# Loading a transformer block's condition and beta as rows and spreading them with TensorE products

## Chip, cores and metric

The kernel runs on one core of a Trainium2 chip. The metric is the device time of one execution in microseconds (us). The core has five engines that run side by side, each in its own order: TensorE (PE in the profile, its weight loads PEld), VectorE (DVE), ScalarE (ACT), GpSimd (POOL) and SyncE (SP). SP and ScalarE also issue DMA transfers; these issues stand in the timeline as SPq and ACTq, and the transfers of the two queues run on the core's 16 DMA engines as q1 (SP) and q10 (ScalarE).

## The reference

A transformer block over 2048 rows of 512 features, with adaptive layer norms. A condition `c` of 512 numbers gives six vectors of 512 that shift, scale and gate the two halves of the block:

```
mod = (silu(c) @ w_mod).reshape(1, 6, 1, 512)     # sa, ca, ga, sb, cb, gb
h = layernorm(x) * (1 + ca) + sa
x = x + ga * A(h)          # 32 heads, 4 segments of 512 rows, softmax attention and a running memory
h = layernorm(x) * (1 + cb) + sb
x = x + gb * ((h @ w_gate) * (h @ w_up)) @ w_down
g = sigmoid(beta)          # inside A: one gate per head, o = g * a_mem + (1 - g) * a_dot
```

So nothing of the attention can be computed before `silu(c)`, its product with the first 1024 columns of `w_mod` (for `sa` and `ca`) and the layer norm of the first segment. `beta`, 32 numbers, is wanted later, when memory and attention are mixed.

## The kernel before, in words

The kernel is one long program without loops on the chip. Attention runs over 4 segments, 4 groups of 8 heads and 2 halves of a group; projections, memory updates and the second half of the block are woven between the attention steps. TensorE's order is written by hand: `MM` (line 84) and `TP` (line 87) chain every product and transpose to the one before. VectorE and ScalarE have such chains too in the opening part: what is called through `CV` and `CA` (line 90) keeps the order of the program text; the profile gives all of these line 39. `pin` ties a DMA or an operation to TensorE's last instruction in the same order, without a wait.

The change lies in the opening part, which runs once. In the order of the text:

- Line 628: ScalarE issues the load of the condition. The host has laid `c` out as 128 rows of 4 (line 1670), and it arrives as a tile `s_c` of 128 partitions by 4 columns, 16 bytes for each partition.
- Line 643: SP issues the first four tiles of `x`, 128 by 512 each. Line 665: it issues the first half of the modulation weights, four tiles `wm0` of 256 KB (`wm0_load(0)`); the second half follows by `wm0_load(1)` (line 1103), after the first key weights (line 759). Line 774 issues four tiles of value weights.
- Lines 648 to 657: 18 products of 512 columns of a tile of zeros, `wu`, into the PSUM tile `wups`, which nobody reads: work that warms TensorE up. `wups` has two banks; the products fill the first.
- Line 669: ScalarE issues the load of `beta`, spread by the DMA over all 128 partitions, 128 bytes to each, into `be`.
- Lines 670 to 673: silu. ScalarE computes exp(-c); VectorE adds 1, takes the reciprocal and multiplies by c, in place in `s_c`.
- Line 675: four fills on GpSimd of rows of the tiles `kst`, tied behind the last of these operations.
- `gates` (line 677) uses `be` for the two sigmoids, `gg` and `omg`. Line 680 is its exponential on ScalarE.
- `ln` (line 172): for each of four tiles of `x` VectorE computes statistics (`bn_stats`) and joins them (`bn_aggr`, line 182); then follow two operations on ScalarE, four small ones on VectorE, and the normalisation of the four tiles. Sixteen transposes on TensorE (line 209, by way of line 88) put the result in PSUM as `atp`.
- `mod0` (line 719) multiplies the modulation weights by `s_c`, four blocks of 128 columns and four parts of the condition, with the moving column repeated 96 times (`MW`); an f32 product is two instructions. `mod0(0)` stands on TensorE ahead of the transposes, `mod0(1, (1, 2, 3))` behind them; the latter takes its first two parts as one sum that ScalarE (line 1109) and VectorE (line 1112) make beforehand.
- Then `a_kq` computes the first keys and queries (`kps`, `qps`), and the block proper begins.

Storage that is used by turns goes by tags: a tile that takes a tag whose buffer is in use waits for the last reader. The tags `mem` and `pkr` of the pool `pa`, one buffer each, serve the value weights in this part and parts of the memory update later.

Of the kernel before, what the change touches and what calls it, by code (L numbers as in the profile page):

```python
# [8 lines left out]
F32 = mybir.dt.float32  # L9
F32R = mybir.dt.float32r  # L10
BF = mybir.dt.bfloat16
AF = mybir.ActivationFunctionType
# [5 lines left out]
P = 128  # L18
S, D, H, DH, NSEG, L, F = 2048, 512, 32, 16, 4, 512, 1376
KT = D // P  # L20
# [6 lines left out]
ONES2 = 1.0 + 0x3F80 / 2.0 ** 23  # L27
SYNC = mybir.DependencyInfo(mybir.DependencyClass.Sync, mybir.DependencyReason.DATA)
# [29 lines left out]
def tile_kernel(ctx, tc, x, wq, wk_, wv, wo, beta, w_gate, w_up, w_down, c, w_mod, out):  # L58
    nc = tc.nc
# [3 lines left out]
    def open_pool(**kw):  # L63
        p = tc.tile_pool(**kw)
        return p, p.__enter__()
# [6 lines left out]
    def pe(i):  # L72

        if last_pe[0] is not None:
            tc.add_manual_dep(i.ins, last_pe[0].ins.name, NOSYNC, reason="order")
        last_pe[0] = i
        return i

    def pin(i):

        if last_pe[0] is not None:
            tc.add_manual_dep(i.ins, last_pe[0].ins.name, NOSYNC, reason="order")

    def MM(*a, **k):
        return pe(nc.tensor.matmul(*a, **k))  # L85

    def TP(*a):
        return pe(nc.tensor.transpose(*a))

    CV, CA = Chain(tc, nc.vector), Chain(tc, nc.scalar)  # L90
    vec, act = Switch(nc.vector), Switch(nc.scalar)
# [35 lines left out]
    def bank(name, dt=F32, shape=(P, 512), small=False):  # L127

        flush()
        rest_of()  # L130
        nbank[0] += 1
        tag = btag[nbank[0] % len(btag)]
        if tag == "ms":
            if not small:
                nlast[0] ^= 1
            tag = f"ms{nlast[0] ^ int(small)}"
        return pst(shape, tag, name, dt)
# [4 lines left out]
    ones = cst.tile([P, P], F32, name="ones")  # L142
# [14 lines left out]
    s_c = cst.tile([P, KT], F32, name="s_c")  # L157
    be = cst.tile([P, H], F32, name="be")
    e1 = cst.tile([P, KT], F32, name="e1")
# [12 lines left out]
    def ln(pool, hpool, xt, s, sc, sh, pfx, hb, fast):  # L172

        first = pfx == "a" and s == 0
        V, A = (CV, CA) if first else (vec, act)
        mv = pool.tile([P, 4, 2], F32, tag="mv", name=f"{pfx}mv{s}", bufs=2)
        for t in range(4):
            st = pool.tile([P, 6], F32, tag="st", name=f"{pfx}st{s}_{t}", bufs=2)
            i = V.bn_stats(st, xt[t])
            if not first:  # L180
                pin(i)
            V.bn_aggr(mv[:, t, :], st)
            if not first:
                yield 0.0
        sd = pool.tile([P, 4], F32, tag="sd", name=f"{pfx}sd{s}", bufs=2)
        A.activation(sd, mv[:, :, 1], AF.Ln, bias=epst[:, 0:1])
        y = pool.tile([P, 4], F32, tag="y", name=f"{pfx}y{s}", bufs=2)
        A.activation(y, sd, AF.Exp, scale=-0.5)
        a = pool.tile([P, 4], F32, tag="ya", name=f"{pfx}ya{s}", bufs=2)
        b = pool.tile([P, 4], F32, tag="yb", name=f"{pfx}yb{s}", bufs=2)  # L190
        eng = CV if first else nc.gpsimd
        eng.tensor_mul(a, y, y)
        if first:
            CV.scalar_tensor_tensor(b, mv[:, :, 1], EPS, a, op0=ALU.add, op1=ALU.mult)
        else:
            eng.tensor_scalar(b, mv[:, :, 1], 1.0, EPS, op0=ALU.mult, op1=ALU.add)
            eng.tensor_mul(b, b, a)
        eng.tensor_scalar(b, b, -0.5, 1.5, op0=ALU.mult, op1=ALU.add)
        eng.tensor_mul(y, y, b)
        yield 0.0  # L200
        tps = [bank(f"{pfx}tp{s}_{d}") for d in range(KT)] if first else []
        for t in range(4):
            i = V.tensor_scalar(xt[t], xt[t], mv[:, t, 0:1], y[:, t:t + 1],
                                op0=ALU.subtract, op1=ALU.mult)
            if not first:
                pin(i)
                yield 0.0
            for d, ps in enumerate(tps):
                TP(ps[:, t * P:(t + 1) * P], xt[t][:, d * P:(d + 1) * P], ident)
        if first:  # L210
            yield 0.0
        hH, hL = [], []
        if first:
            hcur[0] = hH, hL
        for d in range(KT):
            if first:
                ps = tps[d]
            else:
                ps = bank(f"{pfx}tp{s}_{d}", small=pfx == "c" and s == 0)
                for t in range(4):  # L220
                    TP(ps[:, t * P:(t + 1) * P], xt[t][:, d * P:(d + 1) * P], ident)
            h = pool.tile([P, L], F32, tag="hf", name=f"{pfx}hf{s}_{d}", bufs=hb[2])
            A.activation(h, ps, AF.Identity, scale=sc[:, d:d + 1], bias=sh[:, d:d + 1])
            hi = hpool.tile([P, L], F32R, tag=hb[0].format(d), name=f"{pfx}hH{s}_{d}", bufs=hb[1])
            lo = hpool.tile([P, L], F32R, tag=hb[0].format(4 + d), name=f"{pfx}hL{s}_{d}", bufs=hb[1])
            if fast:
                if d % 2:
                    A.activation(hi, h, AF.Copy)
                else:
                    V.tensor_copy(hi, h)  # L230
                V.tensor_sub(lo, h, hi.bitcast(F32))
            else:
                act.activation(hi, h, AF.Copy)
                nc.gpsimd.tensor_sub(lo, h, hi.bitcast(F32))
            hH.append(hi)
            hL.append(lo)
            yield 0.45
            if pfx == "a" and not first and d % 2 == 1:
                yield False
        return hH, hL  # L240
# [18 lines left out]
    kst = [ap.tile([98, HQ, L], BF, name=f"kst{i}") for i in range(NB)]  # L259
# [365 lines left out]

    pwpool, pw = open_pool(name="pw", bufs=1, reuse_waits="tile")
    papool, pa = open_pool(name="pa", bufs=2, reuse_waits="tile")
    nc.scalar.dma_start(s_c, c)
    wm = w_mod.rearrange("(k p) n -> p k n", p=P)

    def load_mod(i):
# [7 lines left out]
    def xload(s):  # L639
        xt = []  # L640
        for t in range(4):
            a = pa.tile([P, D], F32, tag="x", name=f"x{s}_{t}", bufs=4)
            pin(nc.sync.dma_start(a, x[rows(s, t), :]))
            xt.append(a)
        return xt

    xts = {0: xload(0)}
    NWU = 18
    wu = pa.tile([P, 512], BF, tag="rl", name="wu", bufs=1)
    vec.memset(wu, 0.0)  # L650
    wups = psp.tile([P, 2, 512], F32, tag="lk", name="wups", bufs=1)

    def warm(n):
        for i in range(n):
            MM(wups[:, 0], wu[:, 0:P], wu, start=True, stop=True)

    warm(NWU)
    wm0 = []
    for k in range(KT):
        a = ap.tile([P, 2, 2, 256], F32, tag="pt", name=f"wm0_{k}", bufs=PT)  # L660
# [5 lines left out]

    wm0_load(0)
    r0 = [[a[:, j].rearrange("p i c -> p (i c)") for a in wm0] for j in range(2)]
    nc.scalar.dma_start(be, beta[None, :].to_broadcast([P, H]))
    act.activation(e1, s_c, AF.Exp, scale=-1.0)  # L670
    CV.tensor_scalar_add(e1, e1, 1.0)
    CV.reciprocal(e1, e1)
    scl = CV.tensor_mul(s_c, s_c, e1)
    for a in kst:
        tc.add_manual_dep(nc.gpsimd.memset(a[96:98].rearrange("p h t -> p (h t)").bitcast(F32), ONES2).ins, scl.ins.name, SYNC, reason="order")

    def gates():

# [50 lines left out]
    def a_ln(s):  # L729
        return ln(pa, pa, xts.pop(s), s, ca_c, sa_c, "a", ("h", 8, 2), s == 0)  # L730
# [373 lines left out]
    next(lw[1])  # L1104
    next(lw[2])
    lng = ln(pa, pa, xts.pop(0), 0, ca_c, sa_c, "a", ("h", 8, 2), True)
    next(lng)
    mod0(0)
# [447 lines left out]
    for f, tag in ((0, "bh7"), (1, "bl7"), (LAST, "bh4")):  # L1556
        a = pc.tile([P, 2, L], F32, tag=tag, name=f"q0_{f}", bufs=1)
# [53 lines left out]
    for n in range(NU):  # L1611
        p, nm, i = units[n]
# [69 lines left out]
```

## Time and profile before

| what | us |
|---|---|
| three runs | 853.75, 854.21, 854.20 (median 854.2) |
| the profiled execution, its own time | 854.15 |
| span in its profile, from the first instruction to the last | 852.4 |

The page lists for each engine the busy time and its share of the span, and a chain of work that ended last. A line of the timeline has the start in the span, the length, the engine, the line of the kernel, the operation, what is written and read, and a count; in brackets stands how long the engine had idled before it and what it had waited for. A line of merged instructions has the length of all of them. DMA lines name the transfer, the issuing queue, how often, the size of each and the median time from issue to landing. Rows by stretch give the length, the busy time and count of each engine, TensorE's granted clock, the share of the DMA engines and GB/s.

### The profile page before, as it was taken

The numbers are of one execution on the slowest core, as the hardware profiler recorded it, in microseconds if no ns is written. First come the engines' busy times: TensorE is split into PE (matmuls) and PEld (weight loads), VectorE is DVE, ScalarE is ACT, GpSimd is POOL, SyncE is SP. The second block draws the span as 40 slices with busy tenths as digits, with TensorE's granted clock in tenths as the row PEclk, the third lists the DMA queues.
The fourth block names the chain that finished last, engine by engine and source line by source line (L and its number), as shares of the span: only waits on it lengthen the run. The fifth ranks groups of instructions, "written<-read, shape, count | busy, mean of one in ns | idle before, by whom it ended". The sixth has DMA issues, their size and how long they took to land.

```text
span 852.4 us, 14404 instructions
## 1 busy us (share of the span) xinstructions
PE 835.3 (98%) x4972; PEld 597.4 (70%) x4972; DVE 643.1 (75%) x1797; ACT 499.0 (59%) x760; POOL 276.8 (32%) x423
## 2 busy tenths in 40 slices
PE   9989999999999999999999999999999999999998
PEld 6756656666665656666665687888888778888886
DVE  7897768887778967787888359989987855447654
ACT  4758767787676876677545626344435555555330
POOL 2756627566565774675434610000000000000000
PEclk9999999999999999999999999999999999999999
DMA  9645435563545554466675466587650685335102
GB/s 271 155 152 155 121 104 141 158 179 115 143 106 166 144 165 106 122 170 213 195 216 155 145 192 230 189 287 271 253 201 28 234 271 210 121 135 184 43 8 98
DMA packets 83928, 139.57 MB, mean 164 GB/s; under 512 B 12720, under 2 KB 46768, under 8 KB 83856
## 3 DMA queue, kind: packets, MB, share of 16 engines
q1 hardware_dynamic: 83424, 138.51, 52.0%
q8 instruction: 39, 0.64, 0.3%
q14 instruction: 33, 0.27, 0.1%
q10 hardware_dynamic: 432, 0.15, 0.1%
HBM read 89.87 MB, written 48.50 MB: 162 GB/s over the span
## 4 chain that ended last, share of the span: by engine, by line
PE 61%; DVE 5%; ACT 1%; issue 0%; POOL 0%; DVEq 0%
PE acc L1358 14%; PE Xg L1289 7%; PE Xu L1289 6%; PE wops L85 5%; PE tb L85 5%; PE Yu L1289 4%; PE Yg L1289 4%; PE k L85 3%; PE q L85 3%; DVE q L39 2%; PE Zg L1289 1%; PE Zu L1289 1%; PE qps L85 1%; PE vps L85 1%; PE Xx L1289 1%; PE up L85 1%
## 5 line engine op out<-in xcount | busy, mean ns | idle before, releaser
L39 DVE CUSTOM_DVE_ANT_0 q<-q,cmask 128x384 f32<-128x384 f32 (+3 forms) x512 | 248.2, 503 | 71.1 <-PE q L85 63.5
L335 ACT ACTIVATE pt<-k 128x1024 f32<-128x1024 f32 x160 | 164.0, 1025 | 74.2 <-PE k L85 71.4
L341 POOL TENSOR_SCALAR_AFFINE_SELECT pt<-pt 128x256 f32<-128x256 f32 (+1 forms) x224 | 98.0, 452 | 137.2 <-ACT pt L335 136.9
L85 PE MATMUL q<-kst,qst 96*128 96x384 bf16 (+3 forms) x512 | 122.8, 302 | 6.5 <-DVE nm L39 5.1
L85 PE MATMUL k<-qst,kst 98*128 98x384 bf16 (+3 forms) x512 | 96.0, 299 | 1.6 <-ACT pt L335 1.3
L1366 DVE TENSOR_TENSOR xa<-xa,acc 128x512 f32<-128x512 f32 x95 | 64.9, 684 | 39.6 <-PE acc L1358 37.8
L85 PEld LDWEIGHTS <-qst 96*128 96x128 bf16 x512 | 43.9, 98 | 58.4 <-issue 43.6
L85 PE MATMUL tb<-pt,v 128*32 128x512 f32 (+3 forms) x1024 | 75.5, 436 | 0.0
L39 DVE DVE_READ_ACCUMULATOR2_ANT nm<- 128x1 f32 x512 | 71.8, 140 | 0.0
L85 PEld LDWEIGHTS <-kst 98*128 98x128 bf16 x512 | 44.4, 98 | 24.9 <-issue 8.8
L1358 PE MATMUL acc<-dH,mH 128*128 128x512 f32 (+1 forms) x152 | 60.3, 397 | 0.0
L1358 PE MATMUL acc<-dL,mH 128*128 128x512 f32 (+1 forms) x152 | 60.1, 395 | 0.0
L1358 PE MATMUL acc<-dH,mL 128*128 128x512 f32 (+1 forms) x152 | 60.0, 395 | 0.0
L85 PEld LDWEIGHTS tb<-pt,v 128*32 128x32 f32 x1024 | 28.7, 109 | 38.6 <-issue 35.7
L367 ACT ACTIVATE tsb<-tb 128x512 f32<-128x512 f32 x32 | 19.1, 596 | 31.6 <-PE tb L85 31.5
L1358 PEld LDWEIGHTS acc<-dH,mL 128*128 128x128 f32 (+1 forms) x152 | 28.5, 188 | 7.1 <-DVE mL L1309 0.3
L1358 PEld LDWEIGHTS acc<-dL,mH 128*128 128x128 f32 (+1 forms) x152 | 28.6, 188 | 7.0
L1358 PEld LDWEIGHTS acc<-dH,mH 128*128 128x128 f32 (+1 forms) x152 | 28.5, 188 | 6.8
L85 PE MATMUL kps<-ahH,wkH 128*128 128x512 f32 x64 | 29.4, 460 | 0.0
L85 PE MATMUL qps<-ahH,wqH 128*128 128x512 f32 x64 | 28.7, 448 | 0.2 <-DVE oL L39 0.2
L85 PE MATMUL vps<-wvH,ahH 128*128 128x512 f32 x64 | 28.3, 442 | 0.0
L85 PE MATMUL wops<-woH,oH 128*128 128x512 f32 x64 | 28.3, 442 | 0.0
(403 smaller groups left out, 2019.1 us busy)
## 6 DMA issues: line engine op xcount, KB each, us to landing
wm<-in_w_mod_dram SPq DMA_DIRECT2D x24, 256.0 KB, 3.9
kd<-k SPq DMA_DIRECT2D x16, 384.0 KB, 2.5
qd<-q SPq DMA_DIRECT2D x16, 384.0 KB, 3.5
kst<-kd SPq DMA_DIRECT2D x32, 192.0 KB, 3.2
qst<-qd SPq DMA_DIRECT2D x32, 192.0 KB, 3.7
x<-in_x_dram SPq DMA_DIRECT2D x16, 256.0 KB, 4.8
kst<-kd SPq DMA_DIRECT2D x32, 128.0 KB, 3.2
qst<-qd SPq DMA_DIRECT2D x32, 128.0 KB, 3.7
```

The costliest lines, as they stand in the source:

```text
L39: i = getattr(self.eng, name)(*a, **k)
L85: return pe(nc.tensor.matmul(*a, **k))
L335: ex = act.activation(pt, kp, AF.Exp, scale=0.25)
L341: sels[u, i] = nc.gpsimd.affine_select(w, w, pattern=[[0, w.shape[1]], [1, P]], compare_op=ALU.is_ge, fill=0.0, base=0, channel_multiplier=-1)
L367: act.activation(tsbs[u], tbs.pop(u), AF.Copy)
L1289: pe(nc.tensor.matmul(ps[0:n], a, b[:, k], start=first and c == 0, stop=last and c == 5, skip_group_check=True))
L1358: pe(nc.tensor.matmul(ps, a[0:m, t * P:(t + 1) * P], b[0:m], start=j == 0, stop=j == n - 1))
L1366: vec.tensor_add(xa, xa, ps)
```

## The change

The host hands the condition over as one row of 512. Condition and beta are loaded as one row each, into one partition. Of the 18 warm-up products 3 stay ahead and 7 behind five new products: four with one row of weights turn the condition's row into four columns (`cps`), one spreads beta's row over the partitions (`bps`), all into the second bank of `wups`. ScalarE's exponential reads `cps` and a copy on ScalarE writes `be` from `bps`. The three VectorE operations and the four fills on GpSimd move into a function that the layer norm calls behind the statistics of the first tile.

```diff
@@ ln @@
             V.bn_aggr(mv[:, t, :], st)
+            if first and t == 0:
+                condition()
...
@@ tile_kernel @@
-    nc.scalar.dma_start(s_c, c)
+    crow = pa.tile([P, D], F32, tag="mem", name="crow", bufs=1)[0:1]
+    brow = pa.tile([P, D], F32, tag="pkr", name="brow", bufs=1)[0:1, 0:H]
+    nc.scalar.dma_start(crow, c)
+    nc.scalar.dma_start(brow, beta[None, :])
...
-    NWU = 18
...
-    warm(NWU)
+    warm(3)
+    cps = wups[:, 1, 0:KT]
+    for k in range(KT):
+        MM(cps[:, k:k + 1], crow[:, k * P:(k + 1) * P], ones[0:1, 0:1], start=k == 0, stop=k == KT - 1, skip_group_check=True)
+    bps = wups[:, 1, KT:KT + H]
+    MM(bps, ones[0:1, :], brow, start=True, stop=True, skip_group_check=True)
+    warm(7)
...
-    nc.scalar.dma_start(be, beta[None, :].to_broadcast([P, H]))
-    act.activation(e1, s_c, AF.Exp, scale=-1.0)
-    CV.tensor_scalar_add(e1, e1, 1.0)
-    CV.reciprocal(e1, e1)
-    scl = CV.tensor_mul(s_c, s_c, e1)
-    for a in kst:
-        tc.add_manual_dep(nc.gpsimd.memset(a[96:98].rearrange("p h t -> p (h t)").bitcast(F32), ONES2).ins, scl.ins.name, SYNC, reason="order")
+    act.activation(e1, cps, AF.Exp, scale=-1.0)
+    act.activation(be, bps, AF.Copy)
+
+    def condition():
+
+        CV.tensor_scalar_add(e1, e1, 1.0)
+        CV.reciprocal(e1, e1)
+        scl = CV.tensor_mul(s_c, cps, e1)
+        for a in kst:
+            tc.add_manual_dep(nc.gpsimd.memset(a[96:98].rearrange("p h t -> p (h t)").bitcast(F32), ONES2).ins, scl.ins.name, SYNC, reason="order")
...
@@ kernel @@
-    vals[9] = vals[9].reshape(KT, P).T
+    vals[9] = vals[9].reshape(1, D)
```

## The prediction

> **What bounds the kernel now.** I read the page's busy times and chain first.
>
> ```profile
> span 852.4 us, 14404 instructions
> PE 835.3 (98%) x4972; PEld 597.4 (70%) x4972; DVE 643.1 (75%) x1797; ACT 499.0 (59%) x760; POOL 276.8 (32%) x423
> PE 61%; DVE 5%; ACT 1%; issue 0%; POOL 0%; DVEq 0%
> ```
>
> TensorE is busy 98% of the span and holds most of the chain that ended last. The edit lies ahead of the first key and query products, so the first question is whether TensorE has slack behind them that would swallow a shift. The table of busy time by stretch answers it (length, then busy time of PE, PEld, DVE, ACT, POOL).
>
> ```profile
> 17.00:30.00 13.00, 13.00 (x58) 10.57 (x58) 12.06 (x19) 12.04 (x21) 3.16 (x2) 1.00 0.60 173
> 30.00:60.00 30.00, 27.12 (x140) 18.91 (x140) 26.36 (x85) 17.23 (x27) 21.06 (x31) 1.00 0.70 174
> 60.00:852.00 792.00, 780.12 (x4689) 557.47 (x4687) 592.92 (x1662) 463.13 (x705) 247.26 (x372) 1.00 0.51 161
> ```
>
> From 17 us on TensorE idles 2.9 us up to 60 and 11.9 us in the 792 us after it. Nothing there runs by a fixed clock: every transfer and operation follows from earlier work. I therefore carry a shift of the first key product, at 16.97 us, one for one to the end. The timeline of TensorE shows what stands ahead of it (start, length).
>
> ```profile
> 1.69 6.82 PE L85 MATMUL wups<-wu 128*128 128x512 bf16 x18 [1.69 <-DVE wu L650]
> 8.79 3.78 PE L85 MATMUL m<-s_c,wm 128*128 128x96 f32 x32 [0.27 <-DVE ast L39]
> 12.41 1.91 PE L88 MATMUL atp<-ident,x 128*128 128x128 f32 x16
> 14.27 1.13 PE L85 MATMUL m<-ones,wm 128*128 128x96 f32 x8
> 15.24 1.95 PE L85 MATMUL m<-s_c,wm 128*128 128x96 f32 x16
> 16.97 0.48 PE L85 MATMUL kps<-ahH,wkH 128*128 128x512 f32 x1
> ```
>
> TensorE runs through from 8.79: modulation (32 instructions, 0.118 each), transposes, modulation again, keys. Ahead lie only the 18 warm-up products on a zero tile. So the prologue's start is set by when the modulation at 8.79 may begin. VectorE is named as its releaser, though it has nothing to give it there. The DMA issues show the real one (the first modulation weights were issued at 2.67 and landed 6.0 later, at 8.67).
>
> ```profile
> 2.67 2.38 SPq L665 DMA_DIRECT2D wm<-in_w_mod_dram  x4
> wm<-in_w_mod_dram SPq DMA_DIRECT2D x1, 256.0 KB, 6.0
> ```
>
> Why 6.0? The view of DMA for 0 to 20 us gives GB/s in slices of half a microsecond; then come two stretches of 2 us, 3.5 to 5.5 and 6 to 8 (q1 is SP's queue, q10 ScalarE's).
>
> ```profile
> GB/s 0 0 0 45 115 368 213 86 114 62 90 275 394 395 379 381 385 354 350 335 316 304 335 346 344 352 343 337 323 323 361 385 389 393 356 327 297 313 281 291
> DMA packets 198, 0.18 MB, mean 88 GB/s; under 512 B 118, under 2 KB 118, under 8 KB 198
> q1 hardware_dynamic: 95, 0.16, 25.8%
> q10 hardware_dynamic: 103, 0.01, 3.7%
> DMA packets 619, 0.77 MB, mean 387 GB/s; under 512 B 50, under 2 KB 432, under 8 KB 619
> q1 hardware_dynamic: 616, 0.77, 105.6%
> ```
>
> The stream reaches 368 GB/s, falls to a quarter of that at 3.5 us, and recovers at 5.5 us. In the hole the large packets of SP and the tiny ones of ScalarE go about one to one (95 and 103). ScalarE's two transfers are the condition and beta:
>
> ```profile
> 0.85 0.39 ACTq L628 DMA_DIRECT2D s_c<-in_c_dram  x1
> 1.27 0.45 ACTq L669 DMA_DIRECT2D be<-in_beta_dram  x1
> s_c<-in_c_dram ACTq DMA_DIRECT2D x1, 2.0 KB, 2.8
> be<-in_beta_dram ACTq DMA_DIRECT2D x1, 16.0 KB, 5.2
> ```
>
> The condition is in at 3.65, beta at 6.47: the hole spans just beta's remaining time. That is a coincidence in time, no proof, and a rival below.
>
> **The change, part by part.** *The two transfers.* 128 pieces of 16 bytes and 128 pieces of 128 bytes become one row each. In the hole 0.18 MB moved where 0.77 MB moves later; the missing 0.59 MB at 387 GB/s is 1.5 us. I take this as what everything behind it in SP's queue gains: the first weights land at 8.67 - 1.5 = 7.2. If beta does not cause the hole, the gain is 0. As ScalarE issues both loads either way, SP's issues lose nothing.
>
> *The new products.* Four for the condition and one for beta, two instructions each, so ten. They wait for the rows, and the 7 remaining warm-up products queue behind them, then the modulation. The condition is issued at 0.85; a row takes between the 1.7 of a one-row load between tiles on chip and the 2.8 of the old condition, so it lands at 2.55 to 3.65; I take 3.1. The 3 warm-up products ahead end their issue at 1.69 + 3 x 0.43 = 3.0, by the weight loads' pace, so little is idle. Beta's row lands at 2.97 to 4.07, before its product is due. The nearest priced products are those of the later modulation columns, same weights, one moving column:
>
> ```profile
> qst<-nt SPq DMA_DIRECT2D x64, 4.0 KB, 1.7
> 142.82 0.97 PEld L85 LDWEIGHTS mc<-ones,wm 128*128 128x128 f32 x8
> 6.79 0.15 PEld L85 LDWEIGHTS <-wu 128*128 128x128 bf16 x1 [0.28 <-issue]
> 7.21 0.80 PEld L85 LDWEIGHTS <-wu 128*128 128x128 bf16 x4 [0.28 <-issue]
> ```
>
> Eight in 0.97 is 0.12 each, 1.2 for ten. That is at TensorE's late pace, and the last two rows show two paces: one warm-up product every 0.43 until 7.21, then one every 0.2, though the granted clock reads 1.00 all through. At the early pace the ten would be double, 2.5. I take 1.4, the row's price with a little for the waits, and keep 1.2 to 2.5. So the 7 warm-up products start at 3.1 + 1.4 = 4.5 and end at 4.5 + 7 x 0.43 = 7.5, just behind the weights at 7.2. The modulation starts at 7.5 in place of 8.79: **1.3 us gained**. With the dear products it starts at 8.6, 0.2 gained; with an early row and a fast pace the weights' 7.2 holds, 1.6 gained.
>
> *The pace behind them.* The fast pace came at 7.21, after 5.5 us of unbroken products. Now the dense run begins at 4.5; 5.5 us on is 10.0. From 7.5 to 10.0 the modulation would then run between full pace and half, a loss of 0 to 1.25. I take **0.5 lost**: a fast pace at 7.21 as before, or weight loads that set the pace in both states, cost nothing; only the full wait costs all. [...]
>
> *The condition's arithmetic moves.* VectorE and ScalarE rows:
>
> ```profile
> 3.70 0.20 ACT L670 ACTIVATE e<-s_c 128x4 f32<-128x4 f32 x1 [1.61 <-DMA s_c<-in_c_dram]
> 3.94 0.17 DVE L39 TENSOR_SCALAR e<-e 128x4 f32<-128x4 f32 x1 [1.16 <-ACT e L670]
> 4.43 0.69 DVE L39 BATCH_NORM_STATS2 ast<-x 128x6 f32<-128x512 f32 x1
> 5.16 0.18 DVE L39 BATCH_NORM_AGGREGATE amv<-ast 128x2 f32<-128x6 f32 x1
> 5.84 0.69 DVE L39 BATCH_NORM_STATS2 ast<-x 128x6 f32<-128x512 f32 x1 [0.50 <-DMA x<-in_x_dram]
> 8.77 0.18 DVE L39 BATCH_NORM_AGGREGATE amv<-ast 128x2 f32<-128x6 f32 x1
> 10.35 1.91 DVE L39 TENSOR_SCALAR x<-x,amv,ay 128x512 f32<-128x512 f32 x4
> 4.64 3.62 POOL L675 MEMSET kst<- 2x1024 f32 x4 [2.37 <-DVE s_c L39]
> 26.84 1.84 POOL L765 TENSOR_TENSOR wkL<-wrk,wkH 128x512 fp32r<-128x512 f32 x1 [18.58 <-ACT wkH L39]
> 10.17 2.73 SPq L774 DMA_DIRECT2D wrv<-in_wv_dram  x4
> ```
>
> The three operations took 0.57 (3.94 to 4.51). They go behind the first statistics, and behind them wait the statistics of tiles two to four. The condition's columns are there at about 4.2, ScalarE adds 0.2, VectorE is through at 5.0, and three tiles of 0.88 end at 7.7, against 8.95 now: the normalised tiles come 1.3 earlier. TensorE wants the first at 7.5 + 3.8 + 0.5 = 11.8, while it was due at 10.35 + 0.5 before: cost 0, under cover of the modulation. Without that cover (columns 1.3 later) the tiles come when they do now. ScalarE's copy of beta, 0.2 by its like at 3.70, stands ahead of nothing due before 8.99. GpSimd's four fills of 3.62 start about 5.1, half a microsecond later, and nothing on it follows until 26.8: cost 0. The two rows lie in buffers that value-weight loads on SP take next, issued from 10.17; the products have read them by 4.5, so that SP does not wait.
>
> *A wait that goes.* The second half of the modulation weights:
>
> ```profile
> 12.58 0.72 ACT L39 ACTIVATE wm<-wm,s_c 128x512 f32<-128x512 f32 x1 [3.06 <-DMA wm<-in_w_mod_dram]
> 13.46 0.75 DVE L39 SCALAR_TENSOR_TENSOR wm<-wm,s_c,wm 128x512 f32<-128x512 f32 x1 [0.63 <-DMA wm<-in_w_mod_dram]
> ```
>
> These waits end 1.5 earlier, ahead of TensorE's shift of 0.8; the product at 14.27 followed the second by 0.06 and the transposes idled about 0.2 for it: **0.2 gained**.
>
> Sum: 1.3 - 0.5 + 0.2 = 1.0 us. The profiled execution took 854.15 (span 852.4 and 1.75 around it), 0.05 from the median of 854.2. So 854.2 - 1.0 = **853.2**.
>
> **The rivals.** *Full gain:* the pace costs nothing and the weights' landing at 7.2 sets the start. 1.6 + 0.2, and up to 0.2 more from the 213 GB/s slice that the condition's pieces fill: 1.8 to 2.0, so 852.3. For it: the early pace ended at 7.21 without regard to what is asked of it; against it: five products behind a landing must all be quick.
>
> *The hole is not beta's:* it is the start of the queue itself. Then the weights land at 8.67 as now, the modulation starts at 8.79, any pace is fast by then, time 854.2. For it: the first slices ramp slowly too. Against it: the hole ends with beta.
>
> *Slower, by the pace:* the interruption at 3.0 to 4.5 and products with one column keep TensorE slow past the modulation's start. 32 instructions at 0.236 take 7.6 and not 3.8, the 16 transposes 3.8 and not 1.9: each microsecond at the slow pace behind 7.5 costs 0.5. It eats the gain of 1.5 if the fast pace comes at 10.5 or later; at 14 the loss is 3.25 and the time 854.2 - 1.5 + 3.25 = 855.9. For it: the early state lasted 5.5 us of unbroken work. Against it: the modulation is itself dense. [...]
>
> **How the numbers follow.** Forecast 0.38 (852.0 to 854.0 with its term ends, 0.10 of it under 852.5), full gain 0.28, no hole of beta's 0.12, slow pace 0.22 (0.02 within the bound). Two tenths of a per cent, 1.7 us, is about what a measurement can tell from no change. Faster: 0.10 + 0.28 = 0.38. Same: 0.28 + 0.12 + 0.02 = 0.42. Slower: 0.20. The range runs from the full gain with half a microsecond to spare, 851.8, to the slow pace's price, 855.9.
>
> **What would show it.** The GB/s row holds above 300 from 2.5 us on, with few q10 packets; the first modulation product starts near 7.5; its 32 instructions take 3.8 (fast) or more (slow); statistics end near 7.7; the first key product starts near 16.0. Wrong if the hole stays, if the ten products take 2.5, or if the key product moves and the end does not.

## The result and the profile after

| | before | changed |
|---|---|---|
| median of 5 runs (range), us | 854.2 (852.63 to 854.96) | 857.13 (856.84 to 858.17) |
| ratio to before, 95% interval | | 1.0039 (1.0028 to 1.0050) |
| the profiled execution, us | 854.15 | 856.97 |
| its span, us | 852.4 | 855.3 |
| first modulation product | 8.79 | 9.50 |
| length of its 32 instructions | 3.78 | 5.84 |
| first key product | 16.97 | 19.53 |

The forecast was 853.2, a gain; the kernel became 2.9 us slower, above the upper end of 855.9. The first key product, which was to come 1.0 earlier, comes 2.56 later.

The timeline of the changed kernel shows where (start, length, then in brackets the idle time before and its releaser):

```profile
3.08 1.78 PEld L85 LDWEIGHTS wups<-ones,crow 1*128 1x128 f32 x8 [0.83 <-issue]
4.74 0.54 PEld L85 LDWEIGHTS wups<-brow,ones 1*128 1x128 f32 x2
5.35 3.17 PE L85 MATMUL wups<-wu 128*128 128x512 bf16 x7
8.56 0.17 ACT L679 ACTIVATE e<-wups 128x4 f32<-128x4 f32 x1 [6.46 <-PE wups L85]
8.76 0.17 DVE L39 TENSOR_SCALAR e<-e 128x4 f32<-128x4 f32 x1 [4.34 <-ACT e L679]
9.36 0.68 DVE L39 BATCH_NORM_STATS2 ast<-x 128x6 f32<-128x512 f32 x1
9.50 5.84 PE L85 MATMUL m<-s_c,wm 128*128 128x96 f32 x32 [0.98 <-DVE s_c L39]
13.46 1.91 DVE L39 TENSOR_SCALAR x<-x,amv,ay 128x512 f32<-128x512 f32 x4
15.19 1.91 PE L88 MATMUL atp<-ident,x 128*128 128x128 f32 x16
16.93 1.03 PE L85 MATMUL m<-ones,wm 128*128 128x96 f32 x8
19.53 0.48 PE L85 MATMUL kps<-ahH,wkH 128*128 128x512 f32 x1
```

The products that make the columns end near 5.4, but ScalarE's exponential reads them only at 8.56, right behind the seven warm-up products. VectorE, in order behind it, idles 4.34 us: the condition's arithmetic and the statistics of tiles two to four come after 8.76, and the tiles of `x` are normalised from 13.46, where it was 10.35. TensorE itself stands still for 0.98 us until `s_c` is there. Then its 32 modulation instructions take 5.84 in place of 3.78. Busy time by stretch, of the modulation's instructions alone, shows at what pace (length, then busy time and count of PE, PEld and DVE, the granted clock, DMA share, GB/s):

```profile
10.00:11.00 1.00, 1.00 (x7) 1.00 (x7) 0.00 (x0) 1.00 1.10 337
...
12.00:13.00 1.00, 1.00 (x6) 1.00 (x6) 0.00 (x0) 1.00 1.11 341
13.00:14.00 1.00, 1.00 (x8) 1.00 (x7) 0.00 (x0) 1.00 1.15 324
14.00:15.00 1.00, 1.00 (x12) 1.00 (x11) 0.00 (x0) 1.00 1.05 369
```

A row counts every instruction that runs in it, so one that crosses a boundary counts twice, and the rows read high (46 in all for the 32). Still, six or seven until about 13.7 and twelve behind it is a change of pace by about two, while the granted clock reads 1.00 in every row. The shift of the first key product adds up: 0.71 from the start, 2.06 from the length, 0.22 won back between the transposes and the keys (from 15.19 to 19.53 is 4.34, and from 12.41 to 16.97 it was 4.56). That is 2.55, and 2.56 was measured. The late tiles of `x` cost nothing of their own here, because the slow modulation was not done before 15.2.

One thing went in the forecast's direction. The view of DMA, 0 to 20 us in slices of half a microsecond:

```profile
GB/s 0 0 0 57 127 402 410 164 131 299 305 285 346 373 272 315 381 357 342 329 330 344 348 348 349 332 329 319 370 369 381 385 275 67 140 322 331 308 85 183
```

The hole that lasted from 3 to 5.5 us is down to two slices, where above 300 from 2.5 us on was forecast. Between 3.5 and 4.5 us no packet of ScalarE's queue moves, and what makes these two slices is not shown. The first modulation weights land at 8.0 (issued at 2.70, 5.3 later): 0.7 earlier than before, not 1.5. They no longer hold the modulation up: its idle time names `s_c`.

### The profile page after: what moved, and what is told of

Same layout as the page of the kernel before. It is cut to its first block, busy times and chain, and to the rows that moved or that the text cites. A ratio compares the mean times of both kernels' runs of the same rounds, so it can differ in the third digit from the quotient of the medians.

```text
span 855.3 us, 14406 instructions
## 1 busy us (share of the span) xinstructions
PE 837.1 (98%) x4974; PEld 600.4 (70%) x4974; DVE 642.8 (75%) x1797; ACT 498.5 (58%) x761; POOL 275.6 (32%) x423
## 4 chain that ended last, share of the span: by engine, by line
PE 59%; DVE 4%; ACT 2%; POOL 2%; issue 1%; DMA 0%; DVEq 0%; ACTq 0%; POOLq 0%
PE acc L1371 14%; PE Xu L1302 7%; PE Xg L1302 7%; PE wops L85 5%; PE tb L85 4%; PE Yu L1302 4%; PE Yg L1302 4%; PE k L85 3%; PE q L85 3%; DVE q L39 2%; PE Zg L1302 1%; PE Zu L1302 1%; PE qps L85 1%; PE vps L85 1%; ACT pt L337 1%
```

## The experiments

The theory after reading the two traces: the exponential waits for warm-up products that have nothing to do with it, because they write the same tile `wups`; that wait carries the loss. The rivals: TensorE reports its work late; the products of one row and one column keep TensorE slow; the move of the condition's arithmetic behind the statistics costs; the new loads cost. Medians stand beside those of the kernel before on the same chip (853.46 to 853.57 on the four chips used), ratios have 95% intervals, and the stretches are from each kernel's own profiled run.

### The shared tile

**own_bank**: the products get a PSUM tile of their own, and nothing else changes.

```diff
+    cbk = psp.tile([P, 512], F32, tag="sm", name="cbk", bufs=1)
-    cps = wups[:, 1, 0:KT]
+    cps = cbk[:, 0:KT]
...
-    bps = wups[:, 1, KT:KT + H]
+    bps = cbk[:, KT:KT + H]
```

> The changed kernel, with the five products writing a PSUM tile of their own and not the second bank of the warm-up tile. Theory (ScalarE's exponential waits for the whole warm-up tile, to 8.56, and TensorE runs at the slow pace behind the interruption): the exponential starts near 4.9, s_c is there near 5.7, the modulation starts when the warm-up ends, near 8.35 and not 9.50, its 32 instructions still take more than 4.5 us, the time falls from 857.1 to between 855 and 856.4, still above before. Rival (the pace alone makes the loss, the wait is hidden behind it): the exponential starts earlier but the time stays within 0.4 us of 857.1. Rival (the wait alone): the 32 instructions take 3.8 and the time is 853.8 or less.

854.23 (853.25 to 855.23, 11 runs), ratio 1.0009 (1.0001 to 1.0018), against 1.0039 for the change. Its timeline:

```profile
5.46 0.17 ACT L680 ACTIVATE e<-cbk 128x4 f32<-128x4 f32 x1 [3.37 <-PE cbk L85]
8.31 3.84 PE L85 MATMUL m<-s_c,wm 128*128 128x96 f32 x32
11.99 1.91 PE L88 MATMUL atp<-ident,x 128*128 128x128 f32 x16
16.33 0.48 PE L85 MATMUL kps<-ahH,wkH 128*128 128x512 f32 x1
```

The exponential starts 3.1 us earlier, TensorE has no gap, and the first key product comes 3.2 us earlier than in the changed kernel, 0.64 earlier than before. So the shared tile carries most of the loss, 0.0030 of 0.0039. The expectation had the slow pace stay: more than 4.5 us for the 32 instructions and a time of 855 to 856.4. They took 3.84 here; the profiled run, at 853.59, is one of the faster of the eleven. That the end gains none of the 0.64 is taken up below.

**read_first**: the same tile, but the two reads on ScalarE stand ahead of the seven warm-up products in the text.

```diff
+    act.activation(e1, cps, AF.Exp, scale=-1.0)
+    act.activation(be, bps, AF.Copy)
     warm(7)
...
-    act.activation(e1, cps, AF.Exp, scale=-1.0)
-    act.activation(be, bps, AF.Copy)
```

> The changed kernel, with ScalarE's two readers written ahead of the seven later warm-up products, all in the one shared tile. Theory (the wait goes to the last writer of the tile in the order of the text): the exponential starts near 4.9, the seven products may start up to 0.9 later because they wait for the readers, the time is that of own_bank or up to 0.9 more. Rival (TensorE reports its small products only when the run behind them is through): the exponential still starts near 8.5 and the time stays at 857.1.

857.52 (856.44 to 858.36, 5 runs), ratio 1.0050 (1.0036 to 1.0063): no better than the change, where own_bank's time or up to 0.9 more was expected. The timeline says why:

```profile
2.73 3.05 SPq L787 DMA_DIRECT2D wrv<-in_wv_dram  x3
5.46 0.17 ACT L667 ACTIVATE e<-wups 128x4 f32<-128x4 f32 x1 [3.36 <-PE wups L85]
9.01 0.16 DVE L39 TENSOR_TENSOR s_c<-wups,e 128x4 f32<-128x4 f32 x1 [2.97 <-PE wups L85]
12.85 2.02 PE L85 MATMUL m<-s_c,wm 128*128 128x96 f32 x16 [0.96 <-DMA wm<-in_w_mod_dram]
```

The exponential runs at 5.46, as the theory says; late reporting by TensorE is out. But VectorE's multiply reads `cps` too, stands later in the text, and waits 2.97 for the warm-ups: each reader waits for the last product written into the tile ahead of it in the text. TensorE stood still for 0.99 here too, up to 9.90, and yet its first 16 modulation instructions took 2.00, the fast pace: such a gap alone does not make the modulation slow. The time as such is no clean measure, because the edit also moved three value-weight loads ahead of the modulation weights on SP, and the second half of the modulation then waited 0.96 for its weights.

### The place and the wait, one at a time

**place_alone**: the kernel before, with the condition's arithmetic called behind the statistics of the first tile.

```diff
             V.bn_aggr(mv[:, t, :], st)
+            if first and t == 0:
+                condition()
```

> The kernel before, with the three VectorE operations of the condition and the four fills moved behind the first tile's statistics as in the change; loads and 18 warm-up products as before. Theory (the place costs nothing as long as the columns are there in time): the three operations run between 5.3 and 5.9 in the wait for the second tile, statistics end at 8.9 to 9.0, the modulation starts at 8.8, the time is within 0.3 us of before. Rival (the place itself delays statistics and fills): statistics end 0.5 later or more, and the time is 0.5 or more above before.

853.4 (853.08 to 854.66, 11 runs), ratio 0.9997 (0.9988 to 1.0006). First key product at 16.99. The move costs nothing, as forecast.

**wait_alone**: place_alone, and the exponential waits for the last of the 18 warm-up products.

```diff
-    act.activation(e1, s_c, AF.Exp, scale=-1.0)
+    ex1 = act.activation(e1, s_c, AF.Exp, scale=-1.0)
+    tc.add_manual_dep(ex1.ins, last_warm[0].ins.name, SYNC, reason="order")
```

> place_alone, with ScalarE's exponential of the condition made to wait for the last of the 18 warm-up products; loads, 18 unbroken products and everything else as there. Theory (the change's loss is mostly this wait, through VectorE): the exponential starts near 8.0 to 8.6, statistics two to four run behind it, the normalised tiles are ready 3 us later than in place_alone, the modulation takes 3.8, the time is 1.7 to 2.6 us above before. Rival (the wait costs only what it delays the modulation, 0.7, and the slow pace the rest): 0.5 to 0.9 above before.

854.92 (854.0 to 856.3, 11 runs), ratio 1.0015 (1.0006 to 1.0024); first key product at 18.45.

```profile
8.17 0.20 ACT L674 ACTIVATE e<-s_c 128x4 f32<-128x4 f32 x1 [1.36 <-PE wups L85]
9.04 3.81 PE L85 MATMUL m<-s_c,wm 128*128 128x96 f32 x32 [0.91 <-DVE s_c L39]
13.68 1.94 PE L88 MATMUL atp<-ident,x 128*128 128x128 f32 x16 [0.83 <-DVE x L39]
```

With TensorE already at its fast pace the wait costs 1.5 us, a little less than the 1.7 to 2.6 expected, and in another way than in the changed kernel: the modulation is quick, and now the transposes wait 0.83 for the late tiles of `x`. The forecast's working had thought of columns 1.3 late, at no cost; here the exponential comes 4.5 later than before (8.17 against 3.70).

### TensorE's pace

**before_interrupted**: the kernel before with its 18 warm-up products cut to 3 and 7, and between them five products of the change's shapes on constants.

```diff
-    warm(NWU)
+    warm(3)
+    for k in range(KT):
+        MM(wups[:, 1, k:k + 1], ones[0:1, :], ones[0:1, 0:1], start=k == 0, stop=k == KT - 1, skip_group_check=True)
+    MM(wups[:, 1, KT:KT + H], ones[0:1, :], ones[0:1, 0:H], start=True, stop=True, skip_group_check=True)
+    warm(7)
```

> The kernel before, with its 18 warm-up products replaced by 3, then four products with one row of weights and one with 32 columns on constants that wait for no load, then 7; loads, silu and order are those of before. Theory (the interruption of the dense products delays the fast pace): the modulation starts at 8.8 as before, its 32 instructions take more than 4.5 us and not 3.8, the time is 854.9 to 856.5. Rival (the pace was slow in the changed kernel because TensorE stood idle from 8.5 to 9.5): 3.8 and 854.2.

854.77 (853.71 to 856.9, 11 runs), ratio 1.0021 (1.0013 to 1.0030). The median is 1.3 us above the kernel before, without any wait. In the profiled run, itself at 854.43, the modulation began at 8.66 and took 3.92, not the 4.5 or more expected, so next to nothing of that run's loss came from the pace; half a microsecond came later (below). Four of the eleven runs lie above 856. That these lost their time to the pace is likely, but not shown: none of them left a profile.

**cold_start**: the kernel before with one warm-up product.

```diff
-    NWU = 18
+    NWU = 1
```

> The kernel before with 1 warm-up product in place of 18. Theory (the pace changes about 5 us after dense work begins): the modulation starts at 8.8 and its first instructions follow every 0.23 and not 0.118 until 11 to 14 us; the 32 take 5 to 7 us, the time is 1.5 to 3.5 us above before. Rival (weight loads set the pace in both states): 3.8 to 4.2 us for the 32 and the time of before.

854.91 (854.23 to 855.99, 11 runs), ratio 1.0016 (1.0008 to 1.0025); first key product at 18.66.

```profile
8.66 5.82 PE L85 MATMUL m<-s_c,wm 128*128 128x96 f32 x32 [6.36 <-DVE ast L39]
```

After 6.36 idle microseconds the modulation takes 5.82, as in the changed kernel. This is the price of a slow pace by itself: 2.0 on the modulation, 1.7 at the first key product, 1.45 in the median.

**own_bank_woven**: own_bank with one warm-up product behind each of the condition's four, and three at the end.

```diff
     for k in range(KT):
         MM(cps[:, k:k + 1], crow[:, k * P:(k + 1) * P], ones[0:1, 0:1], start=k == 0, stop=k == KT - 1, skip_group_check=True)
+        warm(1)
...
-    warm(7)
+    warm(3)
```

> own_bank, with one of the later warm-up products behind each of the four condition products and 3 after beta's in place of 7: the same work with shorter breaks, the columns 1.3 us later. Theory (how soon the fast pace comes hangs on how dense the products are): more executions reach the modulation at the fast pace, the runs spread over less than own_bank's 2 us, the time is 0.2 to 0.6 below own_bank. Rival (the breaks do not matter, or the later columns eat it): own_bank's time or up to 0.5 above.

856.53 (855.66 to 857.37, 5 runs), ratio 1.0033 (1.0020 to 1.0046), where a time below own_bank's was expected. Weaving the dense work between the small products keeps neither the pace nor the time:

```profile
7.96 0.17 ACT L681 ACTIVATE e<-cbk 128x4 f32<-128x4 f32 x1 [5.87 <-PE cbk L85]
9.11 5.17 PE L85 MATMUL m<-s_c,wm 128*128 128x96 f32 x32
```

The exponential again waits for beta's product, the last in the tile, and the modulation takes 5.17.

**after_again**: the changed kernel once more, to see how far its pace varies.

> The changed kernel itself, beside the three others on one chip. Theory: wait_alone's loss and a rest of 0.5 to 1.5 us for the slow pace; 2.6 to 3.6 us above before in all. In its profile the exponential again starts when the seventh later warm-up product ends. The modulation's 32 instructions take between 3.8 and 6 us, by the execution.

857.99 (856.69 to 858.86, 5 runs), ratio 1.0047 (1.0034 to 1.0060); the modulation starts at 9.50 again, takes 6.18, and turns fast at about 14.3. All ten runs of the changed kernel lie at 856.69 or above, all eleven of own_bank at 855.23 or below.

### Beta's load and the hole

**beta_late**: the kernel before, with beta's spread load taken from ScalarE's queue and issued by SP behind the opening's loads.

```diff
-    nc.scalar.dma_start(be, beta[None, :].to_broadcast([P, H]))
...
     run(lng)
+    pin(nc.sync.dma_start(be, beta[None, :].to_broadcast([P, H])))
```

> The kernel before, with the spread load of beta issued on SP behind the value weights and not on ScalarE at 1.27; nothing else. Theory (beta's 128 small pieces make the hole in the stream): above 200 GB/s from 3.5 to 5.5 us where 88 was, first weights landed at 7.2 to 8.0, the modulation starts when the 18 warm-up products end, 8.3 to 8.5, the time is 0.3 to 0.5 under before, 853.8; a dip in the stream after 13 us. Rival (the hole is the start of the queue): the hole stays, the modulation starts at 8.8, 854.2.

852.51 (851.72 to 854.15, 11 runs), ratio 0.9991 (0.9982 to 1.0000). The view of DMA for 0 to 20 us, and the timeline:

```profile
GB/s 0 0 0 37 168 256 350 283 328 320 330 377 348 363 371 381 358 324 310 333 346 350 344 350 335 314 319 378 381 385 381 346 307 290 290 292 292 288 273 102
```

```profile
7.42 3.78 PE L85 MATMUL m<-s_c,wm 128*128 128x96 f32 x32
11.97 0.33 SPq L1123 DMA_DIRECT2D be<-in_beta_dram  x1
15.61 0.47 PE L85 MATMUL kps<-ahH,wkH 128*128 128x512 f32 x1
```

No hole, and the first key product comes 1.36 us earlier, although the condition still comes as 128 pieces of 16 bytes. The hole is beta's, and the condition's pieces do no harm. Issued at 11.97, the same load makes no dip, where one was expected: the view has 314 GB/s or more from 12 to 16 us and 290 or more until it lands, 5.4 us after its issue. The gain of 1.0 is more than the 0.3 to 0.5 expected; in the profiled run TensorE turned fast near 5.0 and not at 7.21, so that the 18 warm-up products took 5.67 and not 6.82 and did not hold the modulation up.

**beta_sp_early**: the same load on SP's own queue, right behind the loads of `x`, so that no second queue has large work beside it.

```diff
     xts = {0: xload(0)}
+    pin(nc.sync.dma_start(be, beta[None, :].to_broadcast([P, H])))
...
-    nc.scalar.dma_start(be, beta[None, :].to_broadcast([P, H]))
```

> The kernel before, with the spread load of beta issued on SP between the four tiles of x and the modulation weights. Theory (the hole comes of tiny pieces on a second queue that take turns with the large ones of the first): in one queue the pieces pass in their place, the stream stays above 200 GB/s from 3 to 7 us. Rival (128 reads of the same 128 bytes are slow wherever they stand): a stretch of at least 1.5 us under 150 GB/s between 3.5 and 8.

853.37 in one run. The view of DMA for 0 to 20 us, and the modulation's line:

```profile
GB/s 0 0 0 70 115 302 386 348 385 309 187 82 117 88 250 373 381 387 374 340 303 321 342 344 350 346 340 330 319 337 385 393 381 383 339 308 293 291 289 290
```

```profile
8.57 3.78 PE L85 MATMUL m<-s_c,wm 128*128 128x96 f32 x32 [1.15 <-DMA wm<-in_w_mod_dram]
```

The hole is back, about 1.5 us later and on SP's queue. The expectation's theory, two queues taking turns, is not its cause.

**beta_act_late**: the same load on ScalarE's queue, late.

```diff
-    nc.scalar.dma_start(be, beta[None, :].to_broadcast([P, H]))
...
     CA.activation(r0[1][0], r0[1][0], AF.Copy, scale=s_c[:, 0:1])
+    CA.dma_start(be, beta[None, :].to_broadcast([P, H]))
```

> The kernel before, with the spread load of beta issued on ScalarE's queue behind its scaling of the modulation weights, near 11 to 13 us, while SP's stream still runs; ScalarE's exponential of beta waits for it, so that the time is no measure. Theory (tiny pieces on a second queue): a dip of about 2 us below 200 GB/s after 13 us, where beta_late shows 314 to 350. Rival (only the start of the stream is sensitive): no dip, above 280 GB/s throughout.

857.41 in one run, which, as said in the expectation, is no measure of the load: ScalarE's next operation needs beta and held the engine to 17.72 us. The view of DMA for 13 to 16 us still answers the question:

```profile
DMA packets 880, 1.09 MB, mean 362 GB/s; under 512 B 162, under 2 KB 421, under 8 KB 880
q10 hardware_dynamic: 96, 0.01, 2.5%
```

96 of beta's packets go by while the stream keeps 362 GB/s; the dip that the theory expected is not there. What makes the same 128 reads of 128 bytes dear in the first 8 us and not at 13 stays open.

**beta_late_15**: beta_late with 15 warm-up products, since its 18 ended behind the weights.

```diff
-    NWU = 18
+    NWU = 15
```

> beta_late with 15 warm-up products in place of 18. Theory (with the stream mended, the 18 products set the modulation's start in those executions in which the fast pace comes late): the modulation starts when the weights land, near 7.4, in more of the executions; the time is 0 to 0.6 us under beta_late, 852.0 to 852.5 where before is 853.5. Rival (fewer dense products bring the fast pace later into the modulation): 0.3 us or more above beta_late, and a wider spread.

852.53 (851.8 to 853.02, 11 runs), ratio 0.9986 (0.9977 to 0.9995). The modulation starts at 7.02, when its weights land, and the first key product at 15.40; the two intervals do not tell the time from beta_late's. This and beta_late are the fastest kernels of the study, 1.0 us under the kernel before on the same chip.

### Half a microsecond at 365 us

The copies `tsb<-tb` on ScalarE (32, one for each step of the attention) follow a shift through the kernel. Their starts against the kernel before, in us:

| kernel | first key product | units 0 to 21 | units 22 to 30 | unit 31 |
|---|---|---|---|---|
| wait_alone | +1.48 | +1.17 | +1.15 | +1.18 |
| cold_start | +1.69 | +1.65 | +1.51 | +1.51 |
| beta_late | -1.36 | -1.18 | -1.20 | -0.91 |
| own_bank | -0.64 | -0.55 | 0.00 | +0.29 |
| before_interrupted | -0.14 | -0.20 | +0.30 | +0.31 |
| after | +2.56 | +2.48 | +3.06 | +3.38 |

A shift goes on nearly unchanged through 22 units, but in some kernels half a microsecond is added at unit 22, near 365 us, where the order of the instructions is the same in all of them. There GpSimd waits for the second piece of the output weights (`wor`, 256 KB), which lands 3.6 to 3.7 us after its issue in these kernels and 2.6 to 2.7 in the others. In all seventeen profiles it went with one packet of 16 KB on queue q8, which the profile calls instruction: it began 1.0 to 1.3 us behind the issue of `wor` in the seven kernels with the step, and 2.2 or more in the ten without. The former had 4974 instructions on TensorE, the others 4972 or fewer. Two kernels change that count alone.

**before_20**: the kernel before with 20 warm-up products, which makes 4974.

```diff
-    NWU = 18
+    NWU = 20
```

> The kernel before with 20 warm-up products instead of 18: TensorE issues 4974, as in the changed kernel, and nothing else differs. Transfer theory: packet at 1.0 to 1.2 us behind the issue of the output-weight load, that load lands 1 us later than in before, and the shift against before rises by 0.5 at unit 22; time 0.5 to 0.8 us above before (two more warm-ups put the modulation back by 0 to 0.3). Rival (the small products or the tile cause the jump): packet and landing as before, shift constant, time 0 to 0.3 above before.

**own_bank_5**: own_bank with two warm-up products fewer, which makes 4972.

```diff
-    warm(7)
+    warm(5)
```

> The own-bank kernel with 5 instead of 7 warm-up products behind the condition's, so that TensorE issues exactly as many products as the kernel before (4972 and not 4974). Theory (transfer of instructions): the single packet of 16 KB on the instruction queue, which came 1.0 to 1.2 us behind the issue of the second output-weight load in every kernel that lost half a microsecond at unit 22, and 2.2 us or more behind it in every kernel that did not, moves back to 2.2; that load lands about 2.7 us after its issue and not 3.7, and the shift against before at unit 22 stays that of units 0 to 21 (about -0.5 to -1.0, with modulation starting at 7.5 to 8.3). Time about 0.5 under own_bank's, 853.2 to 853.8. Rival (the products themselves, or the added tile, cause it): the load lands at 3.7, the jump of +0.5 at unit 22 stays, and the time is 853.8 to 854.3.

The view of DMA for 4.4 us from just ahead of the issue has the landing of `wor` (last column: us from issue), first in the kernel before, then in before_20:

```profile
wor<-in_wo_dram SPq DMA_DIRECT2D x1, 256.0 KB, 2.7
```

```profile
wor<-in_wo_dram SPq DMA_DIRECT2D x1, 256.0 KB, 3.6
```

The packet stands in the view of DMA for 362.8 to 363.8 us in the kernel before (`wor` issued at 360.83), and for 361.5 to 362.5 in before_20 (issued at 360.55), as the same line:

```profile
q8 instruction: 1, 0.02, 6.0%
```

And GpSimd's line in the timeline shows who pays for it, first in own_bank, then in own_bank_5:

```profile
364.06 1.29 POOL L971 TENSOR_TENSOR wor<-wor,gab 128x512 f32<-128x512 f32 x1 [1.54 <-DMA wor<-in_wo_dram]
```

```profile
363.53 1.31 POOL L971 TENSOR_TENSOR wor<-wor,gab 128x512 f32<-128x512 f32 x1 [0.45 <-DMA wor<-in_wo_dram]
```

| kernel | TensorE's instructions | packet behind the issue of `wor` | landing of `wor` | shift at unit 21, at unit 22 |
|---|---|---|---|---|
| before | 4972 | 2.2 | 2.7 | |
| before_20 | 4974 | 1.1 | 3.6 | -0.28, +0.25 |
| own_bank | 4974 | 1.0 | 3.7 | -0.59, -0.02 |
| own_bank_5 | 4972 | 2.5 | 2.6 | -0.03, -0.10 |

Two warm-up products more bring the packet close behind the issue and the step into the kernel before; two fewer take both out of own_bank. So the count of instructions is shown as the cause, in both directions; the products' shape and the tile are out. That it is the packet that delays the load is argued from their times: no run moves the packet alone. The medians are too coarse for half a microsecond: before_20 854.25 (ratio 1.0008, 0.9999 to 1.0017), own_bank_5 854.45 (1.0009, 1.0000 to 1.0017), above the 853.2 to 853.8 expected.

own_bank_5 tells something else as well. Its modulation starts at 7.46, where the forecast had it, and yet its first key product is at 16.98, where it was before:

```profile
7.46 5.34 PE L85 MATMUL m<-s_c,wm 128*128 128x96 f32 x32
16.98 0.48 PE L85 MATMUL kps<-ahH,wkH 128*128 128x512 f32 x1
```

**own_bank_2**: own_bank with two warm-up products behind the condition's.

```diff
-    warm(7)
+    warm(2)
```

> The own-bank kernel with 2 instead of 7 warm-up products behind the condition's (TensorE issues 4969). Transfer theory: packet at about 2.4 us behind the issue of the output-weight load, no jump at unit 22. Modulation starts when its weights land, 7.0 to 7.6, at the slow pace for longer, so the first key product is at 15.5 to 16.5 and the time 852.5 to 853.8. If the shorter dense run keeps TensorE slow to 10 us or later after the start of the modulation, the first key product stays at 16.3 or later and the time at 854. Rival (the products cause the jump): +0.5 at unit 22 stays.

855.02 (853.67 to 856.42, 11 runs), ratio 1.0013 (1.0005 to 1.0022), above the 852.5 to 853.8 expected and the 854 named for a longer slow pace, and no step at unit 22.

```profile
7.55 7.01 PE L85 MATMUL m<-s_c,wm 128*128 128x96 f32 x32 [1.17 <-DMA wm<-in_w_mod_dram]
18.74 0.48 PE L85 MATMUL kps<-ahH,wkH 128*128 128x512 f32 x1
```

With so little dense work ahead the modulation runs slow nearly to its end, 7.01. So in these two profiles the change's own gain, the earlier weights, is given back by the pace.

## Why the prediction was wrong, point by point

**The condition's arithmetic: the step that failed.** The prediction put the condition's columns "there at about 4.2", and VectorE "through at 5.0". The products did end near 5.4, but the exponential waited to 8.56, for seven products that share the tile `wups` with the columns and stand ahead of it in the text. The working named what waits behind the products on TensorE; it never asked what the reader of the columns waits for. It priced columns 1.3 later at nothing; VectorE was through with them 4.45 later than it had said (9.29 + 0.16 against 5.0), and TensorE stood still for 0.98. own_bank and read_first show it: a tile of its own brings 3.2 us at the first key product, which leaves it 0.64 earlier than before where 1.0 was forecast, and the wait follows the last writer in the text, reader by reader. The warm-up products fill the first bank of `wups` and the columns lay in its second, and ScalarE waited to 8.56 all the same, against 5.46 in own_bank: the tile decided.

**The price of the ten products.** "I take 1.4", it said, and kept 1.2 to 2.5; it was near the dear end, from 3.08 to 5.35, 2.27 us: f32 weight loads, too, take about twice as long there (8 in 1.78, while 8 of the later ones take 0.97). A mis-sized term, 0.87.

**The start.** 7.5 was forecast and 9.50 came: 0.85 from the products (5.35 against 4.5), 0.17 in the seven warm-ups (3.17 against 3.0), 0.98 from the gap. The weights were not it, though they did not gain the whole 1.5 every time: they landed at 8.0 in the changed kernel and, with the same loads, at 7.5, 7.5, 7.4 and 7.1 in after_again, own_bank, own_bank_2 and own_bank_5, where 7.2 was forecast. The hole was beta's, as said, but the reading that it ends with beta was loose: the stream recovers at 5.5, and beta lands at 6.47.

**The pace.** "I take 0.5 lost"; it was 2.06. In size this is the rival "Slower, by the pace": if a microsecond at the slow pace costs 0.5 (an estimate from the six or seven instructions in a row against twelve), the length of 5.84 means 4.1 us of it, so that the changed kernel turned near 13.6 and after_again near 14.3, where the rival had put 14. Its condition, the interruption, is not enough by itself. In own_bank, whose TensorE order is the same up to 8.3 us but has no gap, the pace turned at about 8.3, and in own_bank_5 only near 10.6. The gap is not enough either, as read_first shows, and no run changes the gap alone. So what sets the moment is not settled. The 5.5 us of unbroken work that the prediction took came from one profile: the other kernels with 15 to 20 unbroken products turned 2.8 to 4.9 us after their first. By the estimate of 0.5 for each slow microsecond the turns came 4.1, 4.8, 4.1 and 6.5 us after the last gap (after, after_again, cold_start, own_bank_2), while read_first was fast at once behind its gap of 0.99 (16 instructions in 2.00).

**The wait that goes.** 0.2 forecast, 0.22 measured.

**One for one to the end.** The step holds through units 0 to 21 to within 0.1 of a microsecond, for shifts from -1.7 to +2.6, though up to 0.3 is lost between the first key product and unit 0 (wait_alone, 1.48 to 1.17). Then a load that lands later, with a packet on the instruction queue beside it, adds 0.6 in the changed kernel, 0.3 is added at unit 31, and the tail gives 0.5 back (855.3 - 852.4 = 2.9 against 3.38). That tail differs by -1.1 to +0.9 between the profiled runs, for no reason that they show, so that at the end one for one holds only to about a microsecond. Net, the 2.56 at the first key product became 2.8 of profiled time.

In sum, 0.85 + 0.17 + 0.98 for the start and 1.56 for the pace are 3.56, and the forecast of -1.0 becomes +2.56 at the first key product, which is what was measured; the rest came later. The prediction had the dear ends of both the products and the pace in its working, but never took them together: 0.2 gained at the start, 1.25 lost by the pace and 0.2 gained by the wait give 855.05, and not the 854.0 at which its forecast ends.

## What to carry to other kernels

Before a result is read early, look at what else writes the tile that holds it: in the shared tile here the reader waited for the last writer ahead of it in the text, even in another bank (to 8.56, and to 5.46 with a tile of its own), and what stands behind the reader on its engine waited too (VectorE 4.34). Small products and gaps ahead of the first dense stretch of TensorE were paid twice in the changed kernel, once as themselves (2.27 and 0.98) and once as a slower stretch behind them (2.06 more on the modulation), and how long that stretch is differed from run to run (5.84 and 6.18 for the same 32 instructions); and the load that blocked the stream was moved behind the loads that are due (0.9991) more cheaply than it was replaced by products (1.0009 at best). An unexplained step far from the edit, half a microsecond near 365 us here, went with one packet of 16 KB on the instruction queue, so compare the time of such a packet with that of the nearest late transfer.

## What the runs showed of the hardware that was not expected

- TensorE's weight loads follow the pace too: an f32 load of 128 columns took 0.22 to 0.27 us before the turn (8 in 1.78, 2 in 0.54) and 0.12 behind it (8 in 0.97), at a granted clock of 1.00 in all rows.
- A load of 256 KB landed 1.0 us later, and the attention behind it 0.5, when one 16 KB packet on the instruction queue began 1.0 to 1.3 us behind its issue and not 2.2 or more. Two more instructions on TensorE, 350 us earlier, were enough for that.
- The step of 0.3 at unit 31 went in the same way with a packet on the other instruction queue, q14: 2.1 to 2.7 us behind an issue of `orl<-od` in the kernels without the step, 3.5 to 3.8 in those with it. No kernel was made to move it alone, so this is a coincidence in time so far.
- 128 reads of the same 128 bytes cut SP's stream for 2 us in the first 8 us, to 88 GB/s on ScalarE's queue (3.5 to 5.5 us) and to 118 on SP's own (5 to 7 us), and not when issued later (352 GB/s from 12 to 15 us and 290 or more until it landed at 17.4 in beta_late, 362 from 13 to 16 in beta_act_late).
